# Two weight blocks moved from a streamed ring into PSUM, in a loop of 64 dependent attention steps

## Chip, cores, metric

One core of one Trainium2 chip. The metric is the device time of one launch in microseconds (us); lower is better. The median of several runs is quoted. Ratios are the mean time of one kernel's fast runs over that of the other's fast runs of the same rounds, so not quite the ratio of the medians.

## The reference, cut to what matters

```python
def _A_ref(x, mem0, Wq, Wk, Wv, Wo, seg_len):      # S = 2048, Dm = 1024, 32 heads of 128, M = 8, seg_len = 32
    mem = mem0
    for s in range(n_seg):                           # 64 steps, each needs mem of the one before
        h = concatenate([mem, x[:, 32*s:32*s+32]], axis=1)          # 40 rows
        q, k, v = h @ Wq, h @ Wk, h @ Wv
        p = softmax(where(mask, q k^T * scale, -1e9))
        o = (p v) @ Wo
        mem = o[:, :M];  outs.append(o[:, M:])
# ... part B: a long convolution by FFT over u, independent of A; the outputs are concatenated
```

The weights are 32 MB in bfloat16 and every step needs all of them. They are 64 blocks of [128, 2048] bfloat16, 512 KB or 4 KB a partition each: 8 blocks (kc 0 to 7) for each of k, q, v and each half t of the heads, and 16 for the output projection. In this text "q 0 4" is the block of q, half 0, kc 4, and "o 8" the output block 8.

## The kernel before

The convolution runs first (some 970 us), then the loop. 46 blocks stay in SBUF ("resident"); 18 are streamed again in every step through a ring of four buffers.

```python
STREAM = {("k", 0): (0, 4), ("q", 0): (0, 4), ("k", 1): (0, 4), ("q", 1): (0, 4), ("v", 0): (0, 4), ("v", 1): (0, 4)}
STREAM_O = (0, 3, 5, 8, 11, 13)
...
wst = ctx_w.enter_context(tc.tile_pool(name="a_wst", bufs=4, side="right"))
def unit(key):
    if key in W_res:
        return W_res[key]
    t_ = wst.tile([128, 2048], BF16, name="wst", tag="w")
    nc.sync.dma_start(out=t_[:], in_=WD[key][:])
    return t_
...
ps_acc = ... bufs=2      # PSUM banks: 2 accumulators, 2 for transposes, 2 for scores and pv, 1, 1 = all 8
...
a = quads("k", 0, range(KC))                     # 4 matmuls of 512 columns for each of 8 blocks
k0 = evac(a, "A")                                # ScalarE copy out of PSUM
a = quads("q", 0, range(KC))
# ... transposes, k 1, scores 0, q 1, softmax 0, v 0, scores 1, v 1, pv 0
oproj(pp[:, 1, :], range(0, 8), o0)              # 8 matmuls of 256 columns for each of 8 blocks
pv1 = pv_x(1, V1, ...); o1 = evac_o(pv1, "B")
oproj(pp[:, 1, :], range(8, 16), o1)
# ... copy out, transpose of the 8 memory rows into hT for the next step, stores
```

The load of a block is issued from the SP queue as soon as its buffer is free, in program order, and a buffer is free when TensorE has used the block that was in it.

## Time and profile before

| | kernel before |
|---|---|
| median | 2944.08 us (2941.65 to 2950.77) |
| loop | 64 steps of 28.84 us |
| weight loads a step | 18 of 512 KB |
| transfer engines in the loop | 0.96 busy, 341 GB/s |

TensorE's longest waits in the 1600 us of the loop between 1100 and 2700 us: the columns are who waited for whom, the total in us, how often, and the longest.

```profile
PE pp L371 <- DMA wst<-WD_o: 159.0, 201, 3.2
PE acc L273 <- DMA wst<-WD_k: 44.8, 72, 1.8
PE acc L273 <- DMA wst<-WD_q: 44.5, 100, 1.9
PE acc L273 <- DMA wst<-WD_v: 40.4, 55, 1.8
```

They add to 288.7 us in 1600 / 28.84 = 55.5 steps, 5.2 us a step.

### The profile page before, as it was taken

To read this page: it belongs to the slowest core of one execution; us is meant where nothing else is said; L and a number is where in the kernel's file an instruction comes from. 1 tells how busy PE (TensorE), PEld (TensorE's weight loads), DVE (VectorE), ACT (ScalarE), POOL (GpSimd) and SP (SyncE) were. 2 spreads that over 40 slices of the span, in tenths; PEclk is the share of its full clock that TensorE was granted. 3 is DMA by queue.
4 is the path that set the end of the run, shared out by engine and by line. 5 is a ranking of instruction groups with operands and counts; after the bars stand their busy time and mean duration, and the time that the engine had idled before them with its cause. 6 is when DMAs were issued, how large, how long until landed. Compare 5 with 4: busy or idle time off the path is not lost.

```text
span 2949.0 us, 75939 instructions
## 1 busy us (share of the span) xinstructions
PE 2124.8 (72%) x32791; PEld 1128.5 (38%) x32838; DVE 1355.8 (46%) x2622; ACT 967.4 (33%) x1394; POOL 599.2 (20%) x993
## 2 busy tenths in 40 slices
PE   1478777846887478777777777777777777777747
PEld 0246444622333244333343333333443333334323
DVE  7577677748983143434333333434333333434320
ACT  4767688731222122222222222222222222222210
POOL 2254435460001111111111111111111111111100
PEclk8689899968899798999899989999899899999978
DMA  4555654534338899999999999999999999999991
GB/s 113 155 156 154 183 164 119 150 115 125 112 128 291 327 348 335 343 338 350 333 352 337 343 332 345 350 345 348 329 336 343 324 353 331 352 339 348 348 322 49
DMA packets 376225, 800.93 MB, mean 272 GB/s; under 512 B 114678, under 2 KB 185334, under 8 KB 373840
## 3 DMA queue, kind: packets, MB, share of 16 engines
q1 hardware_dynamic: 335202, 722.51, 70.8%
q0 software_dynamic: 24912, 51.52, 5.2%
q10 hardware_dynamic: 15774, 22.03, 2.3%
q8 instruction: 257, 4.21, 0.6%
q14 instruction: 80, 0.66, 0.1%
HBM read 742.15 MB, written 67.37 MB: 275 GB/s over the span
## 4 chain that ended last, share of the span: by engine, by line
DMA 43%; PE 20%; issue 20%; DVE 6%; ACT 6%; POOL 5%; SPq 0%; ACTq 0%; POOLq 0%; DVEq 0%
DMA wst<-WD_o 14%; DMA wst<-WD_v 9%; PE acc L273 9%; DMA wst<-WD_k 8%; DMA wst<-WD_q 7%; PE pp L371 2%; PE pe L476 2%; DMA olr<-OLd 1%; ACT sn L859 1%; PE pro L125 1%; POOL us L743 1%; POOL us L744 1%; ACT oT L358 1%; PE tr L284 1%; PE ups L738 1%
## 5 line engine op out<-in xcount | busy, mean ns | idle before, releaser
L273 PEld LDWEIGHTS <-hT 128*32 128x32 bf16 x12288 | 320.7, 100 | 540.1 <-issue 256.7
L273 PE MATMUL acc<-wst,hT 128*32 128x512 bf16 x3072 | 330.2, 415 | 203.2 <-DMA wst<-WD_k 85.2
L279 ACT CAST ev<-acc 128x512 bf16<-128x512 f32 x384 | 225.4, 587 | 528.5 <-PE acc L273 485.8
L371 PEld LDWEIGHTS <-oT 128*32 128x32 bf16 x8192 | 227.8, 102 | 303.3 <-issue 209.8
L371 PE MATMUL pp<-wst,oT 128*32 128x256 bf16 x3072 | 167.0, 296 | 215.8 <-DMA wst<-WD_o 180.7
L285 DVE COPY KT<-tr 128x512 bf16<-128x512 bf16 x128 | 54.4, 425 | 539.8 <-PE tr L284 539.8
L273 PE MATMUL acc<-W_k,hT 128*32 128x512 bf16 x3072 | 249.7, 434 | 0.0
L371 PE MATMUL pp<-W_o,oT 128*32 128x256 bf16 x5120 | 231.5, 294 | 0.0
L273 PE MATMUL acc<-W_q,hT 128*32 128x512 bf16 x3072 | 224.8, 396 | 0.0
L273 PE MATMUL acc<-W_v,hT 128*32 128x512 bf16 x3072 | 212.7, 381 | 0.0
L440 DVE CAST ob<-pp 128x256 bf16<-128x256 f32 x64 | 27.2, 425 | 369.7 <-issue 365.2
L358 ACT CAST oT<-pv 128x512 bf16<-128x512 f32 x128 | 75.3, 588 | 255.7 <-PE pv L345 252.1
L311 DVE TENSOR_REDUCE mx<-sc 128x8 f32<-128x320 f32 x128 | 62.4, 487 | 197.7 <-PE sc L304 197.6
L1033 PE MATMUL yp<-Bt,mi 128*128 128x512 bf16 x379 | 113.8, 405 | 32.3 <-DVE Bt L987 16.3
L951 PE MATMUL hps<-KT,MF 128*128 128x512 bf16 x374 | 100.8, 415 | 49.4 <-DVE x L962 26.1
L252 POOL DMA_DIRECT2D xt<-XTd x64 | 35.9, 561 | 483.9 <-PE pp L345 395.8
L285 ACT COPY QT<-tr 128x512 bf16<-128x512 bf16 x128 | 75.0, 586 | 179.2 <-PE tr L284 141.6
L292 POOL COPY KT<-pk 128x128 bf16<-128x128 bf16 x128 | 38.4, 300 | 462.3 <-PE sc L304 449.4
L450 POOL DMA_DIRECT2D out_dram<-ob x256 | 129.7, 513 | 6.0 <-issue 5.9
L125 PE MATMUL pro<-xTl,wsl 128*128 128x512 bf16 x492 | 113.5, 380 | 8.4 <-DVE ua L740 4.6
L313 ACT ACTIVATE sc<-sc 128x320 f32<-128x320 f32 x128 | 54.0, 422 | 189.0 <-DVE sc L312 157.0
L835 DVE SCALAR_TENSOR_TENSOR nr<-kM,ptt 128x656 f32<-128x656 f32 x128 | 106.1, 829 | 21.5 <-ACT kM L834 18.2
(264 smaller groups left out, 3793.4 us busy)
## 6 DMA issues: line engine op xcount, KB each, us to landing
wst<-WD_o SPq DMA_DIRECT2D x384, 512.0 KB, 5.7
wst<-WD_k SPq DMA_DIRECT2D x256, 512.0 KB, 5.6
wst<-WD_q SPq DMA_DIRECT2D x256, 512.0 KB, 5.3
wst<-WD_v SPq DMA_DIRECT2D x256, 512.0 KB, 5.5
Ud<-ux POOLq DMA_DIRECT2D x16, 1024.0 KB, 5.7
uq<-Ud SPq DMA_DIRECT2D x32, 512.0 KB, 5.5
pk<-PKd POOLq DMA_DIRECT2D x64, 192.0 KB, 5.3
wsl<-in_A_Wk_dram SPq DMA_DIRECT2D x16, 512.0 KB, 4.2
```

Source lines behind the costliest of these rows:

```text
L125: nc.tensor.matmul(a[:], lhsT=w[:, kc, 128 * j:128 * j + 128], rhs=xTl[:, kc, :, :].rearrange("p s k -> p (s k)"), start=(kc == 0), stop=( ...
L273: nc.tensor.matmul(a[32 * g:32 * g + 32, :], lhsT=hT[:, kc, :], rhs=w[:, 512 * g:512 * g + 512], start=(kc == 0), stop=(kc == KC - 1), til ...
L279: nc.scalar.copy(out=q[:], in_=a[:])
L285: eng(out=dst, in_=p[:, i, :, :, :])
L311: nc.vector.tensor_reduce(out=mx[:], in_=sc, axis=AX.X, op=ALU.max)
L358: nc.scalar.copy(out=o[:], in_=p[:].rearrange("p a (g q) -> p a g q", g=4))
L371: nc.tensor.matmul(po[32 * qt:32 * qt + 32, :], lhsT=oT[:, h % 4, (h % 16) // 4, :], rhs=w[:, 1024 * hh + 256 * qt:1024 * hh + 256 * qt + ...
L450: nc.gpsimd.dma_start(out=out_a[r0:r0 + XM, 256 * qt:256 * qt + 256], in_=osb[32 * qt:32 * qt + XM, :])
L476: nc.tensor.matmul(pe[b][n][:], lhsT=ol[b][:, hi, :, :].rearrange("p s k -> p (s k)"), rhs=wos[u][:, 1024 * hh + 512 * n:1024 * hh + 512 * ...
L835: v.scalar_tensor_tensor(out=nrs[e // 4][:, e % 4].rearrange("p f t j -> p f (t j)"), in0=kM[:], scalar=MAGIC, in1=ptv, op0=ALU.subtract, ...
L951: pe.matmul(ps[:], lhsT=MF[:, 4 * rr + mc, cs, 128 * kc:128 * kc + 128], rhs=rhs, start=(i == 0 and mc == 0), stop=(i == 1 and mc == 3))
L1033: pe.matmul(yp[:], lhsT=m_[:, cs, kc, :], rhs=Bt[:, kc, half, j, c_, :], start=(n == 0), stop=(n == 15))
```

## The change

Its intent is to stream less. PSUM work shrinks from eight banks to four; the other four hold two weight blocks (q 0 0 and o 8, two banks each) as raw 32-bit words, and VectorE copies them into a buffer of the ring in every step. So 16 blocks are streamed in place of 18. The four small stores of a step's result become one.

```diff
+KEPT = {("q", 0, 0): 2, ("o", 8): 2}
 ...
+        if key in kept:
+            return ahead_of.pop(key)
         t_ = wst.tile([128, 2048], BF16, name="wst", tag="w")
 ...
-    ps_acc = ctx_l.enter_context(tc.tile_pool(name="a_acc", bufs=2, space=PSUM))
-    ps_tr = ctx_l.enter_context(tc.tile_pool(name="a_tr", bufs=2, space=PSUM))
-    ps_att = ctx_l.enter_context(tc.tile_pool(name="a_att", bufs=2, space=PSUM))
-    ps_s = ctx_l.enter_context(tc.tile_pool(name="a_soft", bufs=1, space=PSUM))
+    ps_acc = ctx_l.enter_context(tc.tile_pool(name="a_acc", bufs=1, space=PSUM))
+    ps_sc = ctx_l.enter_context(tc.tile_pool(name="a_sc", bufs=1, space=PSUM))
+    ps_pv = ctx_l.enter_context(tc.tile_pool(name="a_pv", bufs=1, space=PSUM))
     ps_o = ctx_l.enter_context(tc.tile_pool(name="a_o", bufs=1, space=PSUM))
+    ps_k = ctx_l.enter_context(tc.tile_pool(name="a_keep", bufs=1, space=PSUM))
+    def words(out, in_):
+        nc.vector.tensor_scalar(out=out.bitcast(I32), in0=in_.bitcast(I32), scalar1=0, scalar2=None, op0=ALU.bitwise_or)
 ...
+    def fetch(key):
+        t_ = wst.tile([128, 2048], BF16, name="wst", tag="w")
+        for n in range(2):
+            if n < KEPT[key]:
+                words(t_[:, 1024 * n:1024 * n + 1024], kept[key][n][:])
+            # ... (a half that is not kept would be loaded)
+        ahead_of[key] = t_
 ...
         a = quads("k", 0, range(KC))
+        fetch(("q", 0, 0))
         k0 = evac(a, "A")
 ...
         oproj(pp[:, 1, :], range(0, 8), o0)
+        fetch(("o", 8))
 ...
-        for qt in range(4):
-            nc.gpsimd.dma_start(out=out_a[r0:r0 + XM, 256 * qt:256 * qt + 256], in_=osb[32 * qt:32 * qt + XM, :])
+        nc.gpsimd.dma_start(out=out_a[s * SL:s * SL + SL, :].rearrange("r (q d) -> q r d", q=4), in_=osb)
```

Cut: the loading of the kept blocks at the start, and where q 0, transposes and pv now take a shared bank.

More of the change, by code (lines that the diff above doesn't have):

```diff
@@ L44, in streamed_keys @@
 def streamed_keys():
-    return [(m, t, kc) for (m, t), kcs in STREAM.items() for kc in kcs] + [("o", u) for u in STREAM_O]
+    return [key for key in [(m, t, kc) for (m, t), kcs in STREAM.items() for kc in kcs] + [("o", u) for u in STREAM_O] if KEPT.get(key) != 2]
 def streamed_copies(ctx, tc, src):
@@ L52, in streamed_copies @@
     for key in streamed_keys():
-        t_ = dram.tile([128, 2048], BF16, name="WD_%s" % "_".join(str(i) for i in key))
-        copies.append(lambda t_=t_, key=key: nc.sync.dma_start(
-            out=t_[:].rearrange("e (h d) -> e h d", h=2) if key[0] == "o" else t_[:], in_=src(key)))
+        part = KEPT.get(key, 0)
+        t_ = dram.tile([128, 2048 - 1024 * part], BF16, name="WD_%s" % "_".join(str(i) for i in key))
+        copies.append(lambda t_=t_, key=key, part=part: nc.sync.dma_start(
+            out=t_[:].rearrange("e (h d) -> e h d", d=1024) if key[0] == "o" else t_[:], in_=src(key)[:, part:] if key[0] == "o" else src(key)))
         out[key] = t_
@@ L159 @@
 RESIDENT = [(m, t, kc) for t in range(2) for m in "kq" for kc in range(8)] + [("v", t, kc) for t in range(2) for kc in range(8)] + [("o", u) for u in range(16)]
-RESIDENT = [key for key in RESIDENT if key not in streamed_keys()]
+RESIDENT = [key for key in RESIDENT if key not in streamed_keys() and key not in KEPT]
 class Keys(list):
@@ L238, in part_a @@
     work = ctx_l.enter_context(tc.tile_pool(name="a_work", bufs=1))
-    ps_acc = ctx_l.enter_context(tc.tile_pool(name="a_acc", bufs=2, space=PSUM))
-    ps_tr = ctx_l.enter_context(tc.tile_pool(name="a_tr", bufs=2, space=PSUM))
-    ps_att = ctx_l.enter_context(tc.tile_pool(name="a_att", bufs=2, space=PSUM))
-    ps_s = ctx_l.enter_context(tc.tile_pool(name="a_soft", bufs=1, space=PSUM))
+    ps_acc = ctx_l.enter_context(tc.tile_pool(name="a_acc", bufs=1, space=PSUM))
+    ps_sc = ctx_l.enter_context(tc.tile_pool(name="a_sc", bufs=1, space=PSUM))
+    ps_pv = ctx_l.enter_context(tc.tile_pool(name="a_pv", bufs=1, space=PSUM))
     ps_o = ctx_l.enter_context(tc.tile_pool(name="a_o", bufs=1, space=PSUM))
+    ps_k = ctx_l.enter_context(tc.tile_pool(name="a_keep", bufs=1, space=PSUM))
+    kept, ahead_of = {}, {}
+    def words(out, in_):
+        nc.vector.tensor_scalar(out=out.bitcast(I32), in0=in_.bitcast(I32), scalar1=0, scalar2=None, op0=ALU.bitwise_or)
+    for key, n_ in KEPT.items():
+        t_ = wst.tile([128, 2048], BF16, name="wst", tag="w")
+        nc.sync.dma_start(out=t_[:].rearrange("e (h d) -> e h d", h=2) if key[0] == "o" else t_[:], in_=src(key))
+        kept[key] = [ps_k.tile([128, 512], F32, name="keep", tag="keep%d" % (len(kept) * 2 + n)) for n in range(n_)]
+        for n in range(n_):
+            words(kept[key][n][:], t_[:, 1024 * n:1024 * n + 1024])
+    def fetch(key):
+        t_ = wst.tile([128, 2048], BF16, name="wst", tag="w")
+        for n in range(2):
+            if n < KEPT[key]:
+                words(t_[:, 1024 * n:1024 * n + 1024], kept[key][n][:])
+            else:
+                nc.sync.dma_start(out=t_[:, 1024:2048], in_=WD[key][:])
+        ahead_of[key] = t_
     def load_pk(j):
@@ L268, in quads @@
             if a is None:
-                a = ps_acc.tile([128, 512], F32, name="acc", tag="acc")
+                a = (ps_sc if (m, t) == ("q", 0) else ps_acc).tile([128, 512], F32, name="acc", tag="sc" if (m, t) == ("q", 0) else "acc")
             for kc in kcs:
@@ L287, in new_tr @@
         def new_tr():
-            return ps_tr.tile([128, 2, 4, 4, SL], BF16, name="tr", tag="tr")
+            return ps_o.tile([128, 2, 4, 4, SL], BF16, name="tr", tag="pp")
         def new_kt(t):
@@ L295, in scores @@
         def scores(t, QT, KT):
-            sc = ps_att.tile([128, 2, 4, NK], F32, name="sc", tag="att")
+            sc = ps_sc.tile([128, 2, 4, NK], F32, name="sc", tag="sc")
             nc.tensor.matmul(sc[:], lhsT=ident[:], rhs=mask[:].unsqueeze(2).to_broadcast([128, 2, 4, NK]), start=True, stop=False, skip_group_check=True)
@@ L319, in softmax_b @@
             nc.vector.tensor_tensor(out=ex, in0=ex, in1=bc(mx[:].unsqueeze(2), [128, 8, NK]), op=ALU.mult)
-            pt = ps_s.tile([128, 10, 32], F32, name="pt", tag="pt")
+            pt = ps_pv.tile([128, 10, 32], F32, name="pt", tag="pv")
             nc.vector.transpose(out=pt[:, 0:8, :], in_=ex[:, :, 0:SL])
@@ L349, in new_qt, with pv_x @@
             return work.tile([128, 4, 4, SL], BF16, name="QT", tag="E")
-        def pv_x(t, V, pb, lbs, tag):
-            p = ps_att.tile([128, 4, 128], F32, name="pv", tag="att")
+        def pv_x(t, V, pb, lbs):
+            p = (ps_pv, ps_sc)[t].tile([128, 4, 128], F32, name="pv", tag=("pv", "sc")[t])
             pv(p[:], t, V, pb, lbs)
@@ L413, in part_a @@
         a = quads("v", 1, H0)
-        pv0 = pv_x(0, V0, pb0[:].rearrange("p a b k -> p a (b k)"), [lb0a, lb0b[:]], "A")
+        pv0 = pv_x(0, V0, pb0[:].rearrange("p a b k -> p a (b k)"), [lb0a, lb0b[:]])
         pp = ps_o.tile([128, 2, 256], F32, name="pp", tag="pp")
@@ L431, in part_a @@
         oproj(pp[:, 1, :], range(0, 8), o0)
-        pv1 = pv_x(1, V1, pk[:, 0:512].rearrange("p (a b) -> p a b", a=4), [lb1[:].rearrange("p a k -> p (a k)")], "B")
+        fetch(("o", 8))
+        pv1 = pv_x(1, V1, pk[:, 0:512].rearrange("p (a b) -> p a b", a=4), [lb1[:].rearrange("p a k -> p (a k)")])
         o1 = evac_o(pv1, "B")
@@ L442, in part_a @@
         if s + 1 < NS:
-            pt_o = ps_tr.tile([128, 2, 4, SL], BF16, name="tro", tag="tr")
+            pt_o = ps_pv.tile([128, 2, 4, SL], BF16, name="tro", tag="pv")
             for j in range(2):
@@ L447, in part_a @@
         nc.gpsimd.dma_start(out=OLd[s], in_=ob[:, 1, :])
-        r0 = s * SL
-        for qt in range(4):
-            nc.gpsimd.dma_start(out=out_a[r0:r0 + XM, 256 * qt:256 * qt + 256], in_=osb[32 * qt:32 * qt + XM, :])
+        nc.gpsimd.dma_start(out=out_a[s * SL:s * SL + SL, :].rearrange("r (q d) -> q r d", q=4), in_=osb)
     ctx_w.close()
```

## The prediction

> **What bounds the kernel now.** I read the page of the kernel before from its slices to its chain. The kernel has two parts: a long convolution, then a loop of 64 dependent attention steps.
>
> ```profile
> PE   1478777846887478777777777777777777777747
> DVE  7577677748983143434333333434333333434320
> DMA  4555654534338899999999999999999999999991
> DMA 43%; PE 20%; issue 20%; DVE 6%; ACT 6%; POOL 5%; SPq 0%; ACTq 0%; POOLq 0%; DVEq 0%
> ...
> wst<-WD_o SPq DMA_DIRECT2D x384, 512.0 KB, 5.7
> wst<-WD_k SPq DMA_DIRECT2D x256, 512.0 KB, 5.6
> ```
>
> From the fifteenth slice on the transfer engines are at 9 tenths or more, TensorE at 7 and VectorE at 3 to 4; that stretch is the loop, and transfers hold the largest share of the chain. The issue rows count 384 + 3 x 256 = 1152 weight blocks of 512 KB, 18 a step. The step is timed by the copy that closes it, in the view of the tile hT, and the transfer rate is read in the table of windows:
>
> ```profile
> L446 DVE COPY hT<-tro x63: 191/192/193, 1027.3 to 2815.6; 128x64 bf16<-128x64 bf16 x63
> ```
> ```profile
> 1100.00:2700.00 1600.00, 1219.14 (x23528) 630.47 (x23524) 586.39 (x1499) 385.48 (x719) 255.85 (x553) 0.93 0.96 341
> ```
>
> 63 copies span 62 steps: (2815.6 - 1027.3) / 62 = **28.84 us a step**, and 64 steps are 1846 us, 63% of the 2944. A step moves 18 x 512 KB of weights, 192 KB of pk, 48 of xt, 64 of OLd and 4 x 12 of results: 9568 KB or 9.80 MB, in 28.84 us 340 GB/s. The window says 341 GB/s at a busy share of 0.96, so almost nothing is left of the transfer engines. The chain inside the loop and the queue's own waits show how the four-buffer ring looks at that bound:
>
> ```profile
> 1508.09 5.92 DMA wst<-WD_o
> 1514.01 0.04 issue
> 1514.05 0.43 PE pp L371 x8
> 1514.48 0.02 issue
> 1514.49 5.86 DMA wst<-WD_q
> ```
> ```profile
> SPq L225 <- PE acc L273: 522.3, 768, 3.2
> SPq L225 <- PE pp L371: 222.5, 373, 2.5
> ```
>
> A block lands, TensorE uses it for 0.43 us, its buffer is loaded again at once, and the load takes 6 us because three others share the engines. The wait list says what TensorE itself loses:
>
> ```profile
> PE pp L371 <- DMA wst<-WD_o: 180.7, 231, 3.2
> PE acc L273 <- DMA wst<-WD_k: 85.2, 81, 34.9
> ...
> PE acc L273 <- DMA wst<-WD_q: 48.7, 109, 1.9
> PE acc L273 <- DMA wst<-WD_v: 44.2, 62, 1.8
> ```
>
> Without the one 34.9 us at the loop's start this is 180.7 + 50.3 + 48.7 + 44.2 = 324 us, 5.1 us a step. So the compute of a step, free of these waits, takes about 28.84 - 5.1 = **23.8 us**. That is the second bound, only 17% below the first.
>
> **What the Trainium skill says.** "DMA: Bandwidth & Descriptors", section Specifications, gives a fabric ceiling of 435 GB/s and some 358 GB/s of HBM for a core; the loop's 341 GB/s at 0.96 busy agrees that it is near a limit. Its section "Anatomy of one DMA" gives a fixed cost of about 2 us besides the moving of bytes; here a 512 KB load into wsl in the quieter part lands after 4.2 us, where 512 KB at 341 GB/s would be 1.54, so about 2.6 us are fixed. "PSUM — Partial Sum Buffer", section Specifications, lets VectorE read PSUM in any dtype and DMA not at all, which is why VectorE has to copy. "VectorE: DVE Perf Modes", section "Why PSUM operands drop a tier", gives 1x for 4-byte PSUM operands: 512 elements at the page's 0.96 GHz are 0.53 us plus a start. The trace agrees: 320 float32 from PSUM take 487 ns in the reduction, 512 took 0.68 us in the widest product of the softmax. I estimate 0.6 to 0.68 us for a copy.
>
> **The change part by part.** (1) *Two of 18 streamed blocks (q 0 0 and o 8) come from PSUM.* A step then moves 16 x 512 + 192 + 48 + 64 + 64 = 8560 KB. At an unchanged 340 GB/s it takes 28.84 x 8560 / 9568 = **25.8 us**, 3.04 less.
>
> (2) *VectorE copies them:* 4 copies x 0.65 = 2.6 us a step, against 586.39 / 1600 x 28.84 = 10.6 us busy now. 13 of 26 us is no bound in the mean. The pair for q 0 0 runs right after the copy to hT, while k 0 takes TensorE 2 to 3 us; its buffer (that of o 11) is free by then, so it hides. The pair for o 8 stands behind the last spread of the second softmax. TensorE needs it after the pv product and its 0.59 us eviction (oT); the instruction order shows the two halves awaited singly, so 0.65 us is enough and it just about hides.
>
> (3) *The second accumulator goes.* Three times a step (q 1, v 0, v 1) the first matmul now waits for the eviction of the accumulator before it; the instruction order shows three new waits for ScalarE and no others of weight. An eviction is a row of its own:
>
> ```profile
> L279 ACT CAST ev<-acc 128x512 bf16<-128x512 f32 x384 | 225.4, 587 | 528.5 <-PE acc L273 485.8
> L450 POOL DMA_DIRECT2D out_dram<-ob x256 | 129.7, 513 | 6.0 <-issue 5.9
> ```
>
> It is 0.59 us plus some 0.15 to start. Scores (0.5 us), a transpose (0.35) and scores lie between, so 0.3 + 0.45 + 0.3 = 1.05 us stay. The other sharings (q 0 with scores, transposes with pp, pt with pv) meet long-finished readers. Compute of a step: 23.8 + 1.05 = 24.85 us, up to 25.5 if the softmax's wait for the second pv, which transfers hide now, comes out.
>
> (4) *One store for four:* 3 x 0.51 us of GpSimd issue less a step and 16 KB more; GpSimd is a fifth busy. On the path: nothing.
>
> (5) *Start of the loop:* two kept blocks are loaded ahead of the first stream: 2 x 1.54 = 3.1 us once.
>
> **Sum.** Transfers 25.8, compute 24.85 to 25.5: the two bounds almost meet, where they were 5 us apart, and in a ring of four neither hides the other wholly. Moreover the two kept blocks each hold a buffer from the moment its predecessor leaves until TensorE uses it, about 5 us, and meanwhile only three loads can be in flight. One load alone takes 4.2 us plus about 0.5 of use, 4.7 / 3 = 1.57 us a block against 1.54 that the engines need: just enough, with nothing spare for stalls such as the pv and its eviction (1.2 us) or the tail from the last o block to the next k (1.35). I add **0.7 us** for this, a judgement of half to one such stall. Step 26.5 us; gain 2.34 x 64 = 150 us; 2944 - 150 + 3 = **2797 us**.
>
> **The rivals.** *A: pure transfer bound.* 25.8 us a step, 2944 - 195 + 3 = 2752. For it: the 0.96 busy share, and that a ring of four kept 0.96 through all of today's stalls. Against: compute at 24.85. *B: lost ring depth or compute becomes the bound.* The busy share falls under 0.9, steps of 27.3 to 27.6 us, 2845 to 2865. For it: three loads only just cover the fixed 2.6 us, and o 8 and q 0 0 sit at the two ends of the stretch in which TensorE stalls. Against: mean room per block rises, since 16 loads now have the buffers less about 11 us a step. *C: PSUM serialisation costs more than the transfers save.* It needs 4 us more compute a step; the three new waits can give at most three whole evictions, 2.2 us. Unlikely. *D: clock.* The skill's "TensorE: Matmul & The Clock Gate", section "What's actually happening", has TensorE fall to half clock after an idle window of about 3.4 us; the trace has 0.50 granted in the 2 us after 1516, when k 0 starts. If the o blocks come closer together this may go and give back up to 1.5 us of compute, which helps only if compute bounds.
>
> **Range and chances.** From a little under A (2745, if fewer stretched packets let the rate rise) to B's upper end, 2865, 8 in 10. Over 2% faster means under 2885, a step below 27.9 us: it fails only if more than two thirds of the transfer saving is lost. 0.89 faster, 0.09 same, 0.02 slower.
>
> **What would show it.** 1024 weight loads instead of 1152; the interval of the hT copies near 26.5 us; a transfer busy share in the loop of 0.91 to 0.95 at 330 to 340 GB/s; 256 PSUM copies of some 0.65 us, TensorE hardly waiting for them; new waits of acc for ev near 1 us a step; TensorE's waits for wst falling from 5.1 to 1 to 2.5 us a step. I am wrong if the copies for o 8 turn up as TensorE's wait, if the share falls under 0.9 (B), or if the part before the loop moves.

## More of the kernel before

Medians of the kernel before lay between 2942 and 2953 us on the chips used, so each experiment is compared with the kernel before on its own chip.

No more SBUF is free: a fifth buffer was refused by the build.

## The result

The changed kernel took **2894.44 us** (2892.48 to 2897.19) against 2943.81 (the kernel before, with a fourth run); ratio 0.983, interval 0.981 to 0.985. That is 1.7% faster, a gain of 49 us where 147 were predicted, and 29 us beyond the slow end of the range that was given, 2865. With a threshold of 2% it counts as the same, to which the prediction had given a chance of 0.09.

The same views of the changed kernel follow. First the copy that closes a step, then the row of the table of windows (busy time of TensorE, its weight loads, VectorE, ScalarE and GpSimd, then TensorE's granted clock, the transfer engines' busy share and GB/s):

```profile
L476 DVE COPY hT<-tro x63: 191/192/192, 1030.1 to 2761.3; 128x64 bf16<-128x64 bf16 x63
```
```profile
1100.00:2700.00 1600.00, 1225.31 (x24341) 655.78 (x24341) 748.53 (x1781) 401.61 (x745) 190.52 (x400) 0.95 0.92 316
```

(2761.3 - 1030.1) / 62 = **27.92 us a step**, 0.92 less than before. Over the 62 intervals that is 57 us, and the two profiled spans, 2949.0 and 2895.5 us, differ by 53.5: the gain is all in the loop. 10.5% of a step's bytes are gone, but the rate fell with them, from 341 to 316 GB/s. The transfer engines' busy share fell only from 0.96 to 0.92. The groups show the copies, and the waits in the same stretch of the loop show who holds TensorE up now:

```profile
L252 DVE TENSOR_SCALAR wst<-keep 128x512 int32<-128x512 int32 x256 | 164.2, 682 | 5.9 <-issue 0.9
```
```profile
PE pp L399 <- DMA wst<-WD_o: 120.9, 152, 2.9
PE acc L300 <- DMA wst<-WD_k: 96.5, 111, 2.4
PE acc L300 <- ACT ev L306: 36.6, 148, 0.4
...
PE acc L300 <- DMA wst<-WD_v: 17.4, 23, 1.6
```

The waits for o and v blocks fell, those for k blocks doubled. With 12.7 us for q they are 247.5 us in 57.3 steps, 4.3 us a step, although two loads fewer are made. New waits for the eviction of the one accumulator are 36.6 / 57.3 = 0.64 us a step. The chain of waits around a step's end (start us, us, what) shows which loads are late:

```profile
1531.86 0.43 PE pp L399 x8
1532.29 0.02 issue
1532.31 6.28 DMA wst<-WD_k
1538.58 0.04 issue
1538.62 3.84 PE acc L300 x36
1542.46 0.02 issue
1542.48 5.47 DMA wst<-WD_q
```

The 8 matmuls at 1531.86 are those of o 8, the first kept block. Only when they are done is the next load of k issued, for it takes over the buffer that o 8 was in. It lands 6.28 us later, and TensorE has waited for it. The 36 matmuls after that (four a block) run from k 0 4 to q 0 4, and the next load on the chain takes over the buffer of q 0 4, late because k 0 4 was. **The kept block stands on the chain, not by its copy but by the buffer that it occupies.** The other one, q 0 0, is within those 36: by the order of the queue's instructions the load of q 1 0 follows in its buffer, and it is issued at 1540.96 us, when q 0 0 is done. The order of VectorE's instructions and the timeline tell how long: the buffer of o 8 is the one that v 1 4 leaves at about 1526.2 us, and o 8 leaves it at about 1532.1, 5.9 us later; q 0 0 takes the one that o 11 left at 1505.6 in the step before and leaves it at 1511.9, 6.3 us.

### The profile page after: what moved, and what is told of

It reads as the page before. It is cut to its first block, busy times and chain, and to the rows that moved or that the text cites. A ratio compares the mean times of both kernels' runs of the same rounds, so it can differ in the third digit from the quotient of the medians.

```text
span 2895.5 us, 76117 instructions
## 1 busy us (share of the span) xinstructions
PE 2091.6 (72%) x32838; PEld 1132.7 (39%) x32838; DVE 1516.0 (52%) x2882; ACT 970.1 (34%) x1394; POOL 515.1 (18%) x801
## 4 chain that ended last, share of the span: by engine, by line
DMA 41%; PE 23%; issue 17%; ACT 8%; DVE 6%; POOL 4%; SPq 1%; ACTq 0%; POOLq 0%; DVEq 0%
DMA wst<-WD_k 14%; PE acc L300 12%; DMA wst<-WD_o 12%; DMA wst<-WD_v 5%; DMA wst<-WD_q 5%; PE pp L399 3%; ACT ev L306 2%; PE pe L505 2%; PE pro L128 2%; ACT sn L888 1%; DMA olr<-OLd 1%; ACT oT L386 1%; POOL us L772 1%; POOL us L773 1%; PE ups L767 1%
## 5 line engine op out<-in xcount | busy, mean ns | idle before, releaser
L300 PEld LDWEIGHTS <-hT 128*32 128x32 bf16 x12288 | 332.3, 99 | 540.2 <-issue 271.1
L300 PE MATMUL acc<-wst,hT 128*32 128x512 bf16 x3072 | 320.1, 402 | 239.4 <-DMA wst<-WD_k 103.8
L399 PEld LDWEIGHTS <-oT 128*32 128x32 bf16 x8192 | 219.1, 100 | 252.4 <-issue 170.8
L300 PE MATMUL acc<-W_k,hT 128*32 128x512 bf16 x3072 | 231.7, 407 | 0.0
L399 PE MATMUL pp<-W_o,oT 128*32 128x256 bf16 x5120 | 222.2, 286 | 0.0
L252 DVE TENSOR_SCALAR wst<-keep 128x512 int32<-128x512 int32 x256 | 164.2, 682 | 5.9 <-issue 0.9
```

Source lines behind the costliest of these rows:

```text
L252: nc.vector.tensor_scalar(out=out.bitcast(I32), in0=in_.bitcast(I32), scalar1=0, scalar2=None, op0=ALU.bitwise_or)
L300: nc.tensor.matmul(a[32 * g:32 * g + 32, :], lhsT=hT[:, kc, :], rhs=w[:, 512 * g:512 * g + 512], start=(kc == 0), stop=(kc == KC - 1), til ...
L399: nc.tensor.matmul(po[32 * qt:32 * qt + 32, :], lhsT=oT[:, h % 4, (h % 16) // 4, :], rhs=w[:, 1024 * hh + 256 * qt:1024 * hh + 256 * qt + ...
```

## The experiments

Theories at this point: **R**, the kept blocks hold buffers of the ring; **P**, the shared PSUM banks cost the gain; **V**, VectorE's copies delay others. In the runs called wrong on purpose a resident block is used in place of another; the comparison with the reference passed in these too, so it is too coarse to notice one block, and passing it says little about the weights used.

| run | loads a step | buffers | kept blocks that hold one | us a step | median us | ratio to before |
|---|---|---|---|---|---|---|
| before | 18 | 4 | 0 | 28.84 | 2944 | 1 |
| changed | 16 | 4 | 2 | 27.92 | 2894 | 0.983 |
| no copy, no buffer * | 16 | 4 | 0 | 26.15 | 2789 | 0.944 |
| copy, no buffer * | 16 | 4 | 0 | 26.24 | 2786 | 0.943 |
| buffer, no copy * | 16 | 4 | 2 | 27.65 | 2888 | 0.978 |
| later buffers | 16 | 4 | 2 | 27.75 | 2888 | 0.977 |
| four banks only | 18 | 4 | 0 | 28.86 | 2965 | 1.005 |
| before, five buffers * | 18 | 5 | 0 | 26.04 | 2773 | 0.940 |
| changed, five buffers * | 16 | 5 | 2 | 25.47 | 2743 | 0.930 |
| q 1 0 for o 8 | 16 | 4 | 2 | 28.59 | 2951 | 0.999 |
| changed, five buffers, right result | 17 | 5 | 2 | 26.13 | **2777** | 0.944 |
| before, five buffers, right result | 19 | 5 | 0 | 26.70 | 2815 | 0.958 |
| only q 0 0 kept | 17 | 4 | 1 | 28.60 | 2942 | 1.000 |
| only o 8 kept | 17 | 4 | 1 | 28.48 | 2935 | 0.998 |
| q 1 0 for q 0 0 | 16 | 4 | 2 | 28.54 | 2941 | 0.998 |
| changed, six buffers | 18 | 6 | 2 | 26.43 | 2810 | 0.953 |

The runs marked * are wrong on purpose. The step is worked out in each run from its copies into hT, as above, in one profiled execution; these executions lay up to 14 us, or 0.2 us a step, from the median of their kernel's runs.

### No copy and no buffer

```diff
-            return ahead_of.pop(key)
+            return W_res[STAND_IN[key]]       # ("q", 0, 1) for ("q", 0, 0), ("o", 9) for ("o", 8)
     def fetch(key):
-        ... (buffer and copies)
+        pass
```

Cut: the loading of the kept blocks ahead of the loop, which goes too.

> Wrong result on purpose: the two kept blocks are replaced by resident neighbours, so that they take neither a copy nor a buffer of the ring; 16 loads a step, four PSUM banks of work and the single store as in the changed kernel. Theory R (the kept blocks hold buffers of the four-deep load ring, and the fixed part of each load comes out): a free ring gives nearly the gain that I had predicted, a step of 25.8 to 26.5 us, 2760 to 2800 us. Theory P (the shared PSUM banks cost the gain): as the changed kernel, 2880 to 2900. Theory V (the VectorE copies themselves delay TensorE or the transfers): as theory R.

2789 us, 0.944 (0.939 to 0.948). From its table of windows:

```profile
1100.00:2700.00 1600.00, 1257.96 (x25749) 684.46 (x25740) 641.23 (x1643) 424.50 (x790) 200.82 (x422) 0.97 0.95 337
```

With the same four banks and the same 16 loads the rate is 337 GB/s, where the changed kernel has 316. This is nearly the time that was predicted. P falls: the four banks were there.

### The copies alone

```diff
     def fetch(key):
+        for n in range(2):
+            words(kept[key][n][:], kept[key][n][:])
```

> As the run without copy and buffer (wrong result on purpose), but VectorE does its four copies a step at the same places, in place in the kept PSUM banks. Theory R: within 0.5% of the run without copies, 2760 to 2805 us. Theory V: back at the changed kernel, 2870 to 2900 us. Theory P: 2880 to 2900 in both.

2786 us, 0.943 (0.939 to 0.946). The groups show that VectorE did its four copies a step:

```profile
L253 DVE TENSOR_SCALAR keep<-keep 128x512 int32<-128x512 int32 x256 | 164.6, 688 | 0.0
```

164.6 us more work on VectorE and no time lost. V falls as the cause of the loss. What this run does not test is a copy on which a matmul depends; in the changed kernel TensorE waited for such copies 3.1 us in the 1600 of the loop.

### The buffer alone

```diff
     def fetch(key):
+        t_ = wst.tile([128, 2048], BF16, name="wst", tag="w")
+        nc.vector.memset(t_[:, 0:512], 0.0)
+        ahead_of[key] = t_
 ...
+                held = ahead_of.pop((m, t, kc), None)
-                ... rhs=w[:, 512 * g:512 * g + 512]
+                ... rhs=held[:, 0:512] if held is not None and g == 3 else w[:, 512 * g:512 * g + 512]
```

(and likewise for the output blocks).

> As the run without copy and buffer (wrong result on purpose), but each kept block takes its buffer of the ring at the same place as in the changed kernel, held by a short VectorE memset of a quarter until the block's last matmul. Theory R: the loss is back, 2870 to 2900 us, and the 4 KB packets are stretched again. Theory V: 2760 to 2800. Theory P: 2880 to 2900 as all others.

2888 us, 0.978 (0.974 to 0.982). Its window row:

```profile
1100.00:2700.00 1600.00, 1212.28 (x24614) 652.76 (x24606) 641.39 (x1679) 404.58 (x752) 192.78 (x405) 0.98 0.92 319
```

The loss is back, with the low rate of 319 GB/s. Holding the two buffers costs 27.65 - 26.15 = 1.50 us a step, or 99 us. **R is shown**: the same loads and the same banks, with the two buffers held or not; only a short memset comes with the hold. The packets tell the same: in the packet records of the loop a 4 KB packet of a weight load has a median of 159 ns in each of these runs, but a mean of 181 before, 188 in the changed kernel, 183 without holds and 187 with them. A busy share made of such records counts stretched packets as work.

### Giving the kept blocks their buffers later

```diff
+        stream(("o", 11)); stream(("o", 13))         # cut: stream() allots a buffer and starts the load
+        if s + 1 < NS:
+            stream(("k", 0, 0))
         fetch(("o", 8))
 ...
         a = quads("k", 0, range(KC))
+        stream(("q", 0, 4))
         fetch(("q", 0, 0))
```

> Right result. The kept blocks keep their copies, but take their buffer later in the ring: the loads of o 11, o 13 and the next step's k 0 0 are allotted their buffers ahead of o 8, and that of q 0 4 ahead of q 0 0, so that a kept block gets the buffer that was used last before it. Theory R: more than half of the lost gain comes back, 2800 to 2850 us. Theories P and V: no change from the changed kernel, 2885 to 2900.

2888 us, 0.977 (0.974 to 0.981): some half a per cent better than the changed kernel at best, far from 2800 to 2850. My expectation failed. The order of the instructions shows one reason: the pool hands out the buffer that is released first, so the load of k 0 4 again got the buffer of o 8 and had to wait for it, and the wait for k blocks was 113.9 us in 1600, not less than the changed kernel's 96.5. What I had shortened was how long o 8 holds a buffer, not what stands behind it: in the timeline of one step o 8 takes the buffer that o 5 leaves at about 1532.1 us and leaves it at 1534.3, some 2 us in place of 5.9, and the load of k 0 4 is issued at 1534.36.

### Four banks and the single store alone

```diff
-KEPT = {("q", 0, 0): 2, ("o", 8): 2}
+KEPT = {}
-        fetch(("q", 0, 0))
-        fetch(("o", 8))
```

> Right result. The changed kernel without its kept blocks: PSUM work in four banks and the single store stay, all 18 blocks are streamed. Theory R (buffers): close to the kernel before, 2935 to 2970 us, since the evictions that now show lie beside waits for loads. Theory P (PSUM sharing costs about 1 us a step): 3000 us or more.

2965 us, 1.005 (1.002 to 1.008). The step is (2827.8 - 1038.3) / 62 = 28.86 us, as before:

```profile
L474 DVE COPY hT<-tro x63: 190/192/193, 1038.3 to 2827.8; 128x64 bf16<-128x64 bf16 x63
```

So four banks and the one store cost nothing in a step as long as loads are what is waited for. Most of the half per cent lies ahead of the loop: the first copy into hT comes at 974.1 us here and at 966.0 in the profile before (from another chip), in code that the edit does not touch; in the profiles of all runs it comes between 960.1 and 975.2. I leave it open.

### Five buffers, with one resident block left out

The room of one resident block pays for a fifth buffer; o 10 stands in for o 9, so the number of loads stays.

```diff
-RESIDENT = [key for key in RESIDENT if key not in streamed_keys() ...]
+RESIDENT = [key for key in RESIDENT if key != ("o", 9) and key not in streamed_keys() ...]
-    wst = ...tile_pool(name="a_wst", bufs=4, side="right")
+    wst = ...tile_pool(name="a_wst", bufs=5, side="right")
     def unit(key):
+        key = ("o", 10) if key == ("o", 9) else key
```

On the kernel before:

> Wrong result on purpose: the kernel before with a fifth buffer in the ring, its room taken from resident block o 9, for which o 10 stands in; still 18 loads a step. If the transfer engines are at their limit at 341 GB/s, as I had predicted, a fifth buffer changes nothing: 2930 to 2955 us. If the depth of the ring already bounds the kernel before, the rate rises and it falls to 2780 to 2880 us.

2773 us, 0.940 (0.936 to 0.943). Its window row:

```profile
1100.00:2700.00 1600.00, 1255.09 (x25649) 660.84 (x25642) 638.29 (x1632) 418.61 (x790) 278.30 (x605) 0.98 0.99 376
```

This decides it. The kernel before was **not** at the limit of its transfer engines: with the same 18 loads and one more buffer they move 376 GB/s (the window reaches some 30 us past the end of this loop; up to 2600 us it is 379). A single load does not get faster by this: the medians from issue to landing are 5.9 to 6.8 us by block type here and were 5.3 to 5.9 before. More loads are under way at once. One buffer is worth more than the whole change. On the changed kernel:

> Wrong result on purpose: the changed kernel with a fifth buffer in the same way (o 10 stands in for o 9); 16 loads and two kept blocks a step. Theory R: the loss to the kept blocks' buffers is made up, 2740 to 2800 us, near the run without copy and buffer. Theory P: no change, 2870 to 2900.

2743 us, 0.930 (0.926 to 0.933), a step of 25.47 us. That lies in the 24.85 to 25.5 us that the prediction had worked out for the compute of a step with four banks, but it is not this bound. TensorE still waits for loads (waits between 1100 and 2600 us):

```profile
PE acc L301 <- DMA wst<-WD_k: 40.3, 64, 1.9
PE acc L301 <- DMA wst<-WD_q: 39.3, 48, 2.5
...
PE pp L400 <- DMA wst<-WD_o: 30.7, 55, 1.2
```

With 5.7 us for v they are 116.0 us in 58.9 steps, 2.0 us a step.

### Five buffers honestly, with and without kept blocks

The fifth buffer is paid by one more streamed block: v 1 streams kc 0, 3 and 6 instead of 0 and 4. Results are right.

```diff
-... ("v", 1): (0, 4)}
+... ("v", 1): (0, 3, 6)}
-name="a_wst", bufs=4
+name="a_wst", bufs=5
```

> Right result. The changed kernel with a fifth buffer bought honestly: the resident block pair of v 1 gives way, v 1 streams kc 0, 3 and 6 in place of 0 and 4, so one more load a step (17) and five buffers. Theory R: the ring no longer bounds, the step is near the compute of 24.9 to 25.5 us plus some waiting, 25.5 to 26.5 us, 2750 to 2810 us. If the transfer limit of 341 GB/s were real: 17 loads or 9072 KB would need 27.3 us, 2850 us.

On the changed kernel, 2777 us, 0.944 (0.940 to 0.949), a step of (2655.7 - 1035.6) / 62 = 26.13 us:

```profile
L476 DVE COPY hT<-tro x63: 191/192/193, 1035.6 to 2655.7; 128x64 bf16<-128x64 bf16 x63
```

**This is the best right version found, and beats both kernels.** On the kernel before:

> Right result. The kernel before with the same trade and nothing else: five buffers, 19 loads a step, no block in PSUM. Theory R: at the 376 GB/s that five buffers reached with 18 loads, 10080 KB need 27.4 us a step, 2840 to 2870 us, faster than the changed kernel without using PSUM. If the transfer engines were at their limit at 341 GB/s: 30.3 us, 3030 us.

2815 us, 0.958 (0.954 to 0.962), better than I expected, for its rate went to 388 GB/s:

```profile
1100.00:2700.00 1600.00, 1255.06 (x25482) 662.89 (x25474) 632.57 (x1619) 411.44 (x779) 273.69 (x595) 0.98 1.01 388
```

It streams *more* than the kernel before, uses no PSUM for weights, and is 2.5 points faster than the change. With five buffers the change is worth 0.958 to 0.944; with four it was worth 1 to 0.983.

A sixth buffer, with kc 0, 3 and 6 of v 0 streamed as well, was the last step of this:

> Right result. The changed kernel with six buffers and 18 loads (v 0 and v 1 stream kc 0, 3 and 6). If depth still bounded at five buffers: 2740 to 2765 us. If the ring is deep enough at five and the extra load only costs transfer: 2780 to 2830 us.

2810 us, 0.953 (0.949 to 0.957), so the sixth buffer does not pay for the load that it costs. That it is worth nothing is not shown: the step grew by 26.43 - 26.13 = 0.30 us, while one more load at five buffers (18 to 19, on the kernel before) cost 26.70 - 26.04 = 0.66.

### Which block is kept

Only one of the two:

```diff
-KEPT = {("q", 0, 0): 2, ("o", 8): 2}
+KEPT = {("q", 0, 0): 2}            # or {("o", 8): 2}, and the other fetch taken out
```

> Right result. Only block q 0 0 lives in PSUM, o 8 is streamed again: 17 loads, one held buffer. If both holds cost alike, half of the changed kernel's gain, 2910 to 2930 us. If the hold of o 8 is the dear one, 2870 to 2900.

> Right result. Only block o 8 lives in PSUM, q 0 0 is streamed again: 17 loads, one held buffer. If both holds cost alike, 2910 to 2930 us. If the hold of q 0 0 is the dear one, 2870 to 2900; if that of o 8 is, 2930 to 2950.

2942 us, 1.000 (0.997 to 1.003), and 2935 us, 0.998 (0.994 to 1.001). A load less and a held buffer more cancel. I had expected half the gain from each. Both together gave 1.7%, more than the sum of the two; why is open.

Another block, q 1 0, copied while TensorE works on k 1:

```diff
-KEPT = {("q", 0, 0): 2, ("o", 8): 2}
+KEPT = {("q", 0, 0): 2, ("q", 1, 0): 2}
-        fetch(("o", 8))
         a = quads("k", 1, H0)
+        fetch(("q", 1, 0))
```

> Right result. Block q 1 0 is kept in PSUM in place of o 8, and copied while TensorE works on k 1, in the dense part of the step; o 8 is streamed again, so there are 16 loads as in the changed kernel. Theory R in its sharper form (a buffer is dear where TensorE stalls, just before o 8, since the next load then cannot be issued): 2800 to 2860 us. If a held buffer costs the same anywhere: 2880 to 2900.

2951 us, 0.999 (0.991 to 1.006): nothing gained. I then blamed the two holds for lying close together, and kept q 1 0 with o 8 instead:

> Right result. Blocks q 1 0 and o 8 are kept (q 0 0 streamed again), so the two held buffers lie far apart in the step. Theory R with overlap (keeping q 0 0 and q 1 0 lost all its gain because both held a buffer at once and left a ring of two): near the changed kernel, 2880 to 2910 us. If q 1 0 is simply a bad block to keep: 2930 us or more.

2941 us, 0.998 (0.993 to 1.002). Its window row:

```profile
1100.00:2700.00 1600.00, 1216.47 (x23817) 633.37 (x23812) 725.17 (x1737) 393.26 (x729) 187.03 (x392) 0.95 0.90 309
```

The overlap is not it: with the holds apart the rate is 309 GB/s too. What makes q 1 0 a worse block than the other two is open.

### A ledger of buffer time

One sum orders these runs. Four buffers offer 4 x 28.84 = 115.4 us of buffer time in a step before; 18 loads use it up, **6.41 us each** (free, loaded, waiting, used). Take 6.41 for each streamed load in the other four-buffer runs, and what is left falls to the kept blocks:

| run | 4 x step - loads x 6.41 | for each kept block |
|---|---|---|
| no copy, no buffer | 104.6 - 102.6 = 2.0 | (none held) |
| changed | 111.7 - 102.6 = 9.1 | 4.6 |
| buffer, no copy | 110.6 - 102.6 = 8.0 | 4.0 |
| later buffers | 111.0 - 102.6 = 8.4 | 4.2 |
| only q 0 0 | 114.4 - 109.0 = 5.4 | 5.4 |
| only o 8 | 113.9 - 109.0 = 4.9 | 4.9 |
| q 1 0 for o 8 | 114.4 - 102.6 = 11.8 | 5.9 |
| q 1 0 for q 0 0 | 114.2 - 102.6 = 11.6 | 5.8 |

This is an estimate, and it only puts the measured steps in another form. The 6.41 us is not the same in every run: without holds it is 104.6 / 16 = 6.54. The timeline's 5.9 and 6.3 us for the two holds are the direct reading. As an account of the change it says that a user of a buffer that took 6.4 us was replaced by one that takes 4 to 6, and that only the difference, divided by four buffers, comes off the step. It does not predict: in the run with later buffers o 8 held its buffer some 4 us less by the timeline, which would be 1.0 us a step, and the step was 0.17 us shorter. Where in the step a buffer is missing counts too, and no run here separates that.

## Why the prediction was wrong

- **The bound: wrong, and the root of the miss.** "The window says 341 GB/s at a busy share of 0.96, so almost nothing is left of the transfer engines." The same 18 loads went at 376 GB/s with a fifth buffer, and 19 at 388. The bound was the ring: so many loads could be under way, and no more. The chain excerpt that I showed (a load of 5.92 us, 0.43 of use, the next load of 5.86) was the round of one buffer, and I took its length for queueing at engines that could give no more.
- **Step (1), transfers of 25.8 us at an unchanged rate: right only where the buffers stay free, and there partly by luck.** 26.15 us without holds; in the changed kernel the rate fell to 316 GB/s. A ring of four whose loads each take as long as before gives nearly the same figure, 28.84 x 16 / 18 = 25.6, so the agreement does not speak for the transfer bound.
- **Step (2), the copies: right.** 682 ns each for an estimated 0.6 to 0.68, 256 of them, and no time for them alone. TensorE waited 37.1 us for a kept block once, at the loop's start, where before it waited 34.9 for its first load: 2.2 more, for 3.1 predicted.
- **Step (3), the second accumulator: the waits were there, smaller, and free.** 0.64 us a step for 1.05 predicted, and no effect on the step while loads bound. The compute of 24.85 to 25.5 us a step was not confirmed: the 25.47 with five buffers still holds 2.0 us of waits for loads, and less these, as the prediction reckoned, is 23.5, an estimate.
- **Step (4), the store: nothing, together with the banks, as predicted.**
- **The term for the ring: right in kind, wrong in size.** "I add **0.7 us** for this, a judgement of half to one such stall." It measured 1.50 us (buffer alone against none). I had priced it as a small loss on top of a transfer bound, by asking whether three loads can keep the engines busy, when buffer time was the bound itself. The step was predicted 26.5 and is 27.92: the missing 1.42 us are the 0.8 by which this term was too small, 26.15 - 25.8 = 0.35 by which 16 free loads take longer than the bytes say, and 0.27 between the run with buffers alone and the changed kernel, taken on different chips, which can be scatter (0.2 us a step, see the table) or the copies; no run settles it.
- **The rivals.** B, lost ring depth, was the right one, named with the right two blocks at the two ends of TensorE's stalls, and the transfer share at 0.92 did not fall as low as it said. But its 2845 to 2865 us was still too fast, and I gave it the edge of the range instead of the middle. A was refuted as a bound. C did not occur. D was not tried; the granted clock in the loop was 0.93 before and 0.95 after.
- **The signs.** 1024 loads, the copies, the waits for evictions and the busy share of 0.92 came as said or nearly so. The step, the rate (316 GB/s for 330 to 340) and TensorE's waits for loads (4.3 us a step for 1 to 2.5) did not.

## What to carry to other kernels

In a ring of few buffers, ask what one more buffer gives before asking how to stream less: a busy share near 1 does not show that the transfer engines are at their limit, and trading one resident block for a fifth buffer gave 4.2% here while streaming more. When data is moved out of the stream, count the buffer time that the substitute takes as well as the bytes that it saves; a copy that lands in the same ring saves bytes but hardly any buffer time. The sum buffers x step / loads, compared with the landing time of a load, does not show such a bound by itself: it was 6.41 us against landings of 5.3 to 5.9 with four buffers, and 7.23 against 5.9 to 6.8 with five. The run with one buffer more, even with a wrong result, showed it.

## What the Trainium skill lacked or had wrong

- "DMA: Bandwidth & Descriptors", section Specifications: its row of some 358 GB/s of HBM for a core is no limit for one core at work alone. The loop moved 376 GB/s (18 loads, five buffers) and 388 (19 loads). The same page's section "Measured (HBM→SBUF, 128 partitions, SWDGE, issued from GpSimd)" has 425 GB/s and says below its table that this is one core alone, with half of the pair's bandwidth for each when both stream; I leaned on the wrong row.
- "Perfetto Trace Analysis", section "Identifying the Most-Contended Engine", advises HBM utilization in place of the occupancy of the 16 transfer engines, and I had not followed it. Against the row of 358 GB/s it would have been 341 / 358 = 0.95, an estimate, and would not have shown the room either. What the page lacks is that a busy share made of packet records counts stretched packets: 0.96 at 341 GB/s, 0.99 at 376, 1.01 at 388, with a median of 159 ns for a 4 KB packet in each and means of 181, 170 and 167.
- No page has a duration for a VectorE copy from PSUM to PSUM: a bitwise tensor_scalar of 512 int32 took 688 ns there, against 682 ns from PSUM to SBUF.
- "DMA: Bandwidth & Descriptors", section "Anatomy of one DMA", has the fixed cost of a load issued from GpSimd (those of this ring are issued from SyncE) but no rule for how many buffers hide it; here four were too few (2944 us against 2773 with five), and a sixth did not pay for one more load (2810 us against 2777).
